# Four engines of a fused attention and MLP kernel kept in source order through seven batches, and a store moved by one slot

## The chip, the cores and the metric

The kernel runs on one core of a Trainium2 chip. The metric is the device time of one execution in microseconds (us). TensorE is called PE here, VectorE DVE, ScalarE ACT and SyncE SP, as the profile calls them; PEld is PE's loading of weights, which overlaps its matmuls.

## The reference

For 8 batches of 8 heads, 576 tokens and 64 dimensions, 32 packed queries `p` attend to the keys and values, and then every token attends to the 32 packed results. The heads are put side by side (4608 tokens of 512 values) and go through two MLPs, the first with a maximum of three projections, the second with a softplus.

```python
def sm_attn(qq, kk, vv):
    s = scale * np.matmul(qq, kk.transpose(0, 1, 3, 2))
    a = np.exp(s - np.max(s, axis=-1, keepdims=True))
    return np.matmul(a / (np.sum(a, axis=-1, keepdims=True) + 1e-09), vv)
packed = sm_attn(p, k, v)
x = heads_side_by_side(sm_attn(q, packed, packed))       # (4608, 512)
h = np.maximum(np.maximum(x @ w1, x @ w2), x @ w3)       # (4608, 768)
x = h @ w_out                                            # (4608, 512)
h = x @ w_in                                             # (4608, 2048)
g = np.maximum(h, 0.0) + np.log1p(np.exp(-np.abs(h)))
out = g @ w_out2                                         # (4608, 512)
```

The weights arrive as 64-bit floats and are narrowed to 32 bits on the chip.

## The kernel before

**Products.** A 32-bit operand is split into a high part (ACT, L106) and a low part (DVE, L107), and each product is three matmuls (`three`, L395: high by high, high by low, low by high). `split` is the helper that makes the two parts; its rows carry the names of what is split: `pwhi`/`pwlo` the packed weights, `hhi`/`hlo` the output of layer 1, `wc` the weights of the tail.

**A batch.** The second attention and layer 1 are one product: `packed_weights` (L374, tile `ps_w`, called PW below) multiplies the packed result of a batch by the weights of layer 1, 4 column blocks of 128 at a time (PW 0 to PW 4), and DVE and ACT split them. Then `layer1_unit` multiplies them by the attention weights `a2hi`/`a2lo`. A unit (f, w) is 12 matmuls; w is one of the three projections. ACT copies unit w = 0 out of PSUM (`m`, L418), and DVE takes the maximum with units 1 and 2 (L420). Layer 2 has four parts e, each 36 matmuls over f = 0 to 5, an ACT copy (L452) and a store to `x2d`.

**The slots.** Batches 1 to 7 run in a loop, ten slots each. Slot f = 0 to 5 has the three units of f; slots 6 to 9 have layer 2. Between the units of batch n lies the small work of batch n+1 (`small_work`): the first attention's scores (tiles `ps_s`; DVE takes the row maximum `mx`, L261, and scales it to `ms`, L265; ACT takes the exponential `e`, L270, with its sum, of which DVE makes `sg` and `rc`, L314 and L318), PE's transposes of `e` (tile `ps_e`, L285, copied by ACT to `e1T`, L291), the values (L305), the second attention's scores, and DVE's 32x32 transposes of the keys and queries (L219, L222). All PSUM tiles of the loop come from one pool of four.

**Narrowing.** Batches 1 to 6 also narrow the second MLP's weights, one block of 128 x 512 in each of the slots 0 to 5 (`narrow_ahead`): a load of a 64-bit block (`raw`, L651, three blocks ahead), ACT's `rebase` (L82) and DVE's two steps of `narrow` (L93, L96) into a tile `x` of a pool of three, which `store_narrowed` sends to DRAM from SP (L637).

**Batch 7** has no next batch and no narrowing. Instead it begins the tail (`BATCH_END`): `make_pair` forms sums of a weight block (four DVE steps `wu`, L717), splits them into `wc` (one ACT and one DVE step over 128 x 1792) and stores them to `wic`; `load_x2` and `make_x2` do the like for the first tokens.

**The tail** computes layers 3 and 4 in 9 chunks by 8 pairs (L812, L858 to L860). From the second pair on it reads each pair's `wc` two ahead, from `wic` (`get_pair`, L883).

**Order.** The instructions pass through a scheduler, which chooses each engine's order. PE's is fixed by `pinned`, which makes each step issue after the step before it; SP's transfers are likewise fixed by `in_turn` in the loop. DVE and ACT are free: the scheduler sets their instructions by its own estimates. A slot is written in this order:

```python
if 1 <= slot <= F1:
    layer1_split(n, slot - 1)
...
    for w in range(3):
        small_work(n, 3 * slot + w)
        pinned(layer1_unit, n, slot, w)
...
        transpose_kq(n + ahead, g, which)
...
        in_turn(load_raw, n + ahead, g, which)
store_narrowed()
if 0 < n < B - 1 and slot < F1:
    narrow_ahead()
```

The functions that the diff touches:

Of the kernel before, what the change touches and what calls it, by code (L numbers as in the profile page):

```python
# [19 lines left out]
def packed_attention_maxout_softplus(  # L20
# [35 lines left out]
    F1 = DF1 // P  # L56
# [563 lines left out]
    in_flight, to_store = [], []  # L620
# [4 lines left out]
    def in_turn(fn, *args):  # L625

        if queued:
            with tc.issue_after(queued[-1]):
                fn(*args)
        else:  # L630
            fn(*args)
        queued.append(last_of(mybir.EngineType.SP))

    def store_narrowed():
        while to_store:
            dst, x = to_store.pop(0)
            in_turn(lambda: nc.sync.dma_start(out=dst, in_=x))  # L637

# [24 lines left out]
        9: [("make", 1), ("load", 4), ("load", 5)],  # L663
    }

    for n in range(1, B):
        for slot in range(F1 + KC):

# [15 lines left out]
            for at, ahead, g, which in loads:  # L684
                if at == slot and n + ahead < B:
                    in_turn(load_raw, n + ahead, g, which)
            store_narrowed()
            if 0 < n < B - 1 and slot < F1:
                narrow_ahead()
            if n + 1 == B:  # L690
# [87 lines left out]
                        )(*args)  # L778
                if slot == F1 - 1:
                    wsb_ctx.close()  # L780
    aps_ctx.close()
    a_ctx.close()

# [163 lines left out]
```

## Time and profile before

| | us |
|---|---|
| median of 3 runs (1291.14 to 5892.78) | 1291.52 |
| the profiled execution | 1288.91 |
| its span, from the first to the last instruction | 1287.1 |
| PE busy | 1250.0 (97%) |
| PEld busy | 1127.7 (88%) |
| DVE busy | 719.4 (56%) |
| ACT busy | 458.2 (36%) |

The span's first 121 us hold the loads of the first batches and the whole of batch 0; batches 1 to 7 lie between 121.0 and 528.9, the tail behind that. Batches 1 to 6 repeat with a period of 59.20 us, so one of them is read for all; batch 4, from 298.6 to 357.8, is taken. Times of rows are those of the profiled execution. Spans of instructions that follow each other closely overlap by some hundredths of a microsecond, so that the distance of two starts is a little less than the span.

### The profile page before, as it was taken

To read this page: it belongs to the slowest core of one execution; us is meant where nothing else is said; L and a number is where in the kernel's file an instruction comes from. 1 tells how busy PE (TensorE), PEld (TensorE's weight loads), DVE (VectorE), ACT (ScalarE), POOL (GpSimd) and SP (SyncE) were. 2 spreads that over 40 slices of the span, in tenths; PEclk is the share of its full clock that TensorE was granted. 3 is DMA by queue.
4 is the path that set the end of the run, shared out by engine and by line. 5 is a ranking of instruction groups with operands and counts; after the bars stand their busy time and mean duration, and the time that the engine had idled before them with its cause. 6 is when DMAs were issued, how large, how long until landed. Compare 5 with 4: busy or idle time off the path is not lost.

```text
span 1287.1 us, 23495 instructions
## 1 busy us (share of the span) xinstructions
PE 1250.0 (97%) x9952; PEld 1127.7 (88%) x9952; DVE 719.4 (56%) x1115; ACT 458.2 (36%) x669; POOL 0.7 (0%) x6
## 2 busy tenths in 40 slices
PE   3889999999999999999999999999999999999998
PEld 2679898998989899999999999999999999999997
DVE  3777777786857657686354443544434445444332
ACT  3553434444343434553323323232232222332221
POOL 0000000000000000000000000000000000000000
PEclk7899999999999999999999999999999999999999
DMA  9972848677685724977646556565465554654651
GB/s 263 240 212 91 204 136 231 174 212 193 185 231 171 201 87 166 343 257 266 225 172 225 187 208 214 187 215 212 180 208 203 205 205 172 228 188 180 213 182 58
DMA packets 82121, 255.10 MB, mean 198 GB/s; under 512 B 12128, under 2 KB 47200, under 8 KB 72544
## 3 DMA queue, kind: packets, MB, share of 16 engines
q1 hardware_dynamic: 76240, 242.46, 59.1%
q10 hardware_dynamic: 5776, 11.14, 2.5%
q8 instruction: 78, 1.28, 0.4%
q14 instruction: 27, 0.22, 0.1%
HBM read 211.62 MB, written 41.94 MB: 197 GB/s over the span
## 4 chain that ended last, share of the span: by engine, by line
PE 81%; DVE 2%; DMA 1%; issue 0%; ACT 0%; SPq 0%; DVEq 0%
PE ps L812 28%; PE ps L395 21%; PE acc L860 10%; PE acc L859 10%; PE acc L858 10%; PE ps_w L374 2%; DMA wc<-wic 1%; PE ps_v L305 1%; PE ps_e L285 1%; DVE pwlo L107 1%; DVE mx L261 0%; PE ps_s L246 0%; DVE m L420 0%; DVE x L96 0%; DMA qraw<-in_q_dram 0%
## 5 line engine op out<-in xcount | busy, mean ns | idle before, releaser
L812 PE MATMUL ps<-x2hi,wc 128*128 128x256 f32 x2016 | 370.6, 282 | 0.8 <-DMA wc<-wic 0.8
L812 PEld LDWEIGHTS ps<-x2hi,wc 128*128 128x128 f32 x2016 | 316.1, 190 | 3.9 <-DMA wc<-wic 1.3
L812 PE MATMUL ps<-x2lo,wc 128*128 128x256 f32 x1008 | 283.7, 281 | 0.0
L860 PE MATMUL acc<-w2hi,glo 128*128 128x512 f32 x576 | 224.9, 391 | 0.0
L859 PE MATMUL acc<-w2lo,ghi 128*128 128x512 f32 x576 | 224.8, 390 | 0.0
L858 PE MATMUL acc<-w2hi,ghi 128*128 128x512 f32 x576 | 224.3, 389 | 0.0
L812 PEld LDWEIGHTS ps<-x2lo,wc 128*128 128x128 f32 x1008 | 191.4, 190 | 2.8
L841 ACT ACTIVATE h<-h 128x1024 f32<-128x1024 f32 x72 | 76.3, 1059 | 286.3 <-DVE h L838 286.3
L835 DVE TENSOR_TENSOR h<-h,ps 128x512 f32<-128x512 f32 x72 | 49.5, 687 | 227.8 <-PE ps L812 227.8
L107 DVE TENSOR_TENSOR glo<-h,ghi 128x1024 fp32r<-128x1024 f32 x72 | 88.1, 1223 | 85.1 <-ACT ghi L106 85.0
L395 PE MATMUL ps<-a2hi,pwhi 128*128 128x288 f32 x576 | 129.2, 306 | 2.9 <-DVE pwlo L107 0.9
L860 PEld LDWEIGHTS acc<-w2hi,glo 128*128 128x128 f32 x576 | 108.1, 188 | 23.0 <-DVE glo L107 0.2
L858 PEld LDWEIGHTS acc<-w2hi,ghi 128*128 128x128 f32 x576 | 108.3, 188 | 20.3
L859 PEld LDWEIGHTS acc<-w2lo,ghi 128*128 128x128 f32 x576 | 108.1, 188 | 20.5
L395 PE MATMUL ps<-a2lo,pwhi 128*128 128x288 f32 x576 | 123.8, 297 | 0.3 <-DVE a2lo L107 0.3
L395 PE MATMUL ps<-a2hi,pwlo 128*128 128x288 f32 x576 | 123.6, 296 | 0.0
L395 PEld LDWEIGHTS ps<-a2hi,pwhi 128*128 128x128 f32 x576 | 91.8, 189 | 17.9 <-ACT m L418 5.9
L834 ACT ACTIVATE h<-ps 128x256 f32<-128x256 f32 x72 | 27.5, 382 | 188.0 <-PE ps L812 188.0
L420 DVE TENSOR_TENSOR m<-ps,m 128x576 f32<-128x576 f32 x96 | 72.4, 755 | 38.8 <-PE ps L395 31.4
L395 PEld LDWEIGHTS ps<-a2lo,pwhi 128*128 128x128 f32 x576 | 93.1, 190 | 0.6 <-DVE a2lo L107 0.5
L395 PEld LDWEIGHTS ps<-a2hi,pwlo 128*128 128x128 f32 x576 | 93.0, 190 | 0.2 <-DVE pwlo L107 0.2
L107 DVE TENSOR_TENSOR pwlo<-ps_w,pwhi 128x512 fp32r<-128x512 f32 (+1 forms) x80 | 50.5, 631 | 67.1 <-ACT pwhi L106 66.6
(87 smaller groups left out, 1473.8 us busy)
## 6 DMA issues: line engine op xcount, KB each, us to landing
wc<-wic SPq DMA_DIRECT2D x66, 1792.0 KB
qraw<-in_q_dram SPq DMA_DIRECT2D x112, 140.0 KB
wic<-wc SPq DMA_DIRECT2D x8, 1792.0 KB
kraw<-in_k_dram SPq DMA_DIRECT2D x96, 140.0 KB
wraw<-in_moe_w_dram SPq DMA_DIRECT2D x18, 512.0 KB
x2d<-xs ACTq DMA_DIRECT2D x32, 288.0 KB
xu<-x2d SPq DMA_DIRECT2D x36, 256.0 KB
out_dram<-o SPq DMA_DIRECT2D x136, 64.0 KB
```

The source lines that it names most:

```text
L107: nc.vector.tensor_tensor(out=lo, in0=src, in1=hi.bitcast(F32), op=ALU.subtract)
L285: nc.tensor.transpose(ps[: 32 * TI, i // hi, (i % hi) * P : (i % hi) * P + P], e[:, i], ident,)
L374: nc.tensor.matmul(ps[cols, G, : units * P].rearrange("p (w x) -> p w x", w=units), ppT[n][rows, cols], wsb[rows, 4 * c : 4 * c + units, g ...
L395: nc.tensor.matmul(o, w, xx, start=first, stop=last)
L420: nc.vector.tensor_tensor(out=m, in0=ps[:, :, :HS], in1=ms[n, f], op=ALU.max)
L812: nc.tensor.matmul(out, l, r, start=(i == 0), stop=(i == len(terms) - 1))
L834: nc.scalar.activation(out=h[:, 3], in_=pa[:, 0], func=AF.Copy)
L835: add(out=h[:, 0:5:4], in0=h[:, 3:4].to_broadcast([P, 2, HC]), in1=pb, op=ALU.add)
L841: nc.scalar.activation(out=g, in_=g, func=AF.Softplus)
L858: nc.tensor.matmul(ps, ghi[:, i, cols], whi, start=first, stop=False)
L859: nc.tensor.matmul(ps, ghi[:, i, cols], wlo, start=False, stop=False)
L860: nc.tensor.matmul(ps, glo[:, i, cols], whi, start=False, stop=last)
```

## The change

The loop over batches 1 to 7 is put into a stretch in which the scheduler keeps PE, DVE, ACT and SP in the order in which the program is written. In `store_narrowed`, a block is stored while more than `left` blocks wait: in slots 0 to 5 one stays behind, so that a block narrowed in slot s is stored in slot s+2 rather than s+1, and slot 6 stores what is left.

```diff
-    def store_narrowed():
-        while to_store:
+    def store_narrowed(left):
+        while len(to_store) > left:
             dst, x = to_store.pop(0)
             in_turn(lambda: nc.sync.dma_start(out=dst, in_=x))
...
+    E = mybir.EngineType
+    order_ctx = tc.manual_schedule(engines={E.PE, E.DVE, E.Activation, E.SP})
+    order_ctx.__enter__()
     for n in range(1, B):
         for slot in range(F1 + KC):
...
-            store_narrowed()
+            store_narrowed(1 if slot < F1 else 0)
...
+    order_ctx.__exit__(None, None, None)
```

No instruction is added or removed on any engine. PE's order in the loop stays; 36 of its rows move where the tail begins.

DVE in batch 4, from unit (1,2)'s maximum to the split of PW 3, before:

```order
L420 TENSOR_TENSOR m_3972<-ps_1_3959,m_3910 128x576
L265 TENSOR_SCALAR ms_3954<-mx_3952 128x1
L314 TENSOR_SCALAR sg_4219<-es_3950 128x1
L318 RECIPROCAL rc_4221<-sg_4219 128x1
L107 TENSOR_TENSOR hlo_3989<-m_3972,hhi_3988 128x576
L314 TENSOR_SCALAR sg_4224<-es_3957 128x1
L318 RECIPROCAL rc_4226<-sg_4224 128x1
L420 TENSOR_TENSOR m_4020<-ps_1_4007,m_4005 128x576
L420 TENSOR_TENSOR m_4035<-ps_1_4022,m_4020 128x576
L219 STREAM_TRANSPOSE vT_3974<-qraw_3855 128x576
L107 TENSOR_TENSOR hlo_4046<-m_4035,hhi_4045 128x576
L107 TENSOR_TENSOR pwlo_4050<-ps_w_4051,pwhi_4049 128x512 x2
```

And after:

```order
L420 TENSOR_TENSOR m_3974<-ps_1_3961,m_3912 128x576
L219 STREAM_TRANSPOSE vT_3976<-qraw_3857 128x576
L93 TENSOR_SCALAR raw64_3473<-raw64_3473 128x512
L96 SCALAR_TENSOR_TENSOR x32_3983<-x32_3983,raw64_3473 128x512
L107 TENSOR_TENSOR hlo_3990<-m_3974,hhi_3989 128x576
L420 TENSOR_TENSOR m_4021<-ps_1_4008,m_4006 128x576
L420 TENSOR_TENSOR m_4036<-ps_1_4023,m_4021 128x576
L219 STREAM_TRANSPOSE vT_3976<-qraw_3862 128x576
L93 TENSOR_SCALAR raw64_3548<-raw64_3548 128x512
L96 SCALAR_TENSOR_TENSOR x32_4040<-x32_4040,raw64_3548 128x512
L107 TENSOR_TENSOR hlo_4047<-m_4036,hhi_4046 128x576
L107 TENSOR_TENSOR pwlo_4051<-ps_w_4052,pwhi_4050 128x512 x2
```

Two narrowings (L93, L96) and one more transpose of queries (L219) now stand between that maximum and the split of PW 3, and both row maxima and both `ms` ahead of it; before, these narrowings stood elsewhere in the batch, and `sg` and `rc` here.

ACT at the same place, from the copy of unit (2,0) to that of unit (3,0), before:

```order
L418 ACTIVATE m_4005<-ps_1_3992 128x576
L106 ACTIVATE hhi_4045<-m_4035 128x576
L106 ACTIVATE pwhi_4049<-ps_w_4051 128x512
L291 ACTIVATE e1T_4071<-ps_e_4064 96x768
L106 ACTIVATE pwhi_4049<-ps_w_4051 128x512
L291 ACTIVATE e1T_4080<-ps_e_4073 96x768
L418 ACTIVATE m_4095<-ps_1_4082 128x576
```

And after:

```order
L418 ACTIVATE m_4006<-ps_1_3993 128x576
L82 ACTIVATE x32_4040<-raw64_3548 128x512
L106 ACTIVATE hhi_4046<-m_4036 128x576
L106 ACTIVATE pwhi_4050<-ps_w_4052 128x512 x2
L291 ACTIVATE e1T_4072<-ps_e_4065 96x768
L291 ACTIVATE e1T_4081<-ps_e_4074 96x768
L418 ACTIVATE m_4096<-ps_1_4083 128x576
```

The copy of the first tile of transposes, `e1T`, moved behind the second `pwhi`.

DVE in batch 7, slots 2 and 3, from the last two maxima of slot 2 to the first of slot 3, before:

```order
L420 TENSOR_TENSOR m_6335<-ps_1_6322,m_6320 128x576
L717 TENSOR_TENSOR wu_6220<-wu_6220 128x256 x3
L107 TENSOR_TENSOR hlo_6351<-m_6335,hhi_6350 128x576
L717 TENSOR_TENSOR wu_6220<-wu_6220 128x256
L107 TENSOR_TENSOR pwlo_6355<-ps_w_6356,pwhi_6354 128x512
L107 TENSOR_TENSOR wc_6341<-wu_6220,wc_6341 128x1792
L107 TENSOR_TENSOR pwlo_6355<-ps_w_6356,pwhi_6354 128x512
L420 TENSOR_TENSOR m_6397<-ps_1_6384,m_6382 128x576
```

And after:

```order
L420 TENSOR_TENSOR m_6337<-ps_1_6324,m_6322 128x576
L720 TENSOR_TENSOR wu_6222<-wu_6222 128x256 x4
L107 TENSOR_TENSOR wc_6343<-wu_6222,wc_6343 128x1792
L107 TENSOR_TENSOR hlo_6353<-m_6337,hhi_6352 128x576
L107 TENSOR_TENSOR pwlo_6357<-ps_w_6358,pwhi_6356 128x512 x2
L420 TENSOR_TENSOR m_6399<-ps_1_6386,m_6384 128x576
```

The whole of `make_pair` (L720 is L717 before) now stands ahead of slot 3's splits.

SP's transfers in batch 4, slots 1 to 3 (`wi32` and `wo32` are the stores of narrowed blocks), before:

```order
L157 DMA qraw_3976<-in_q_dram 32x1120 x4
L637 DMA wi32_62<-x32_3870 128x4x128
L651 DMA raw64_3986<-in_moe2_w_out_dram 128x1024
L637 DMA wo32_64<-x32_3982 128x512
L651 DMA raw64_4043<-in_moe2_w_out_dram 128x1024
```

And after:

```order
L157 DMA qraw_3978<-in_q_dram 32x1120 x4
L651 DMA raw64_3987<-in_moe2_w_out_dram 128x1024
L637 DMA wi32_62<-x32_3872 128x4x128
L651 DMA raw64_4044<-in_moe2_w_out_dram 128x1024
L637 DMA wo32_64<-x32_3983 128x512
```

Each store moved behind one more load. Where the tail begins, SP's order changes too: the load of `wc` for pair 2 stands ahead of the loads of layer 4's weights, behind which it stood before, and the DVE part of `make_pair(1)`, which stood at the end of batch 7, stands behind the first drain of layer 3.

## Rows read from the trace of the kernel before

**Rows 1.** The page, busy time, share of the span and instructions of each engine.

```profile
PE 1250.0 (97%) x9952; PEld 1127.7 (88%) x9952; DVE 719.4 (56%) x1115; ACT 458.2 (36%) x669; POOL 0.7 (0%) x6
```

**Rows 2.** Window of batch 4: us, PE, PEld, DVE, ACT, POOL, PEclk, DMA share, GB/s.

```profile
298.60:357.80 59.20, 58.88 (x616) 53.04 (x615) 43.40 (x76) 24.79 (x44) 0.00 (x0) 1.00 0.73 200
```

**Rows 3.** The chain of waits in batch 4: start, us, what.

```profile
317.43 1.02 PE ps_w L374 x16
318.45 1.45 PE ps_e L285 x12
319.89 6.38 PE ps L395 x48
326.28 0.59 PE ps_w L374 x16
326.87 1.48 PE ps_v L305 x96
...
336.62 1.13 PE ps_s L246 x32
```

**Rows 4.** The timeline, batch 4, slots 1 and 2: start, us, engine, [idle before <-releaser].

```profile
309.45 0.42 DVE L93 TENSOR_SCALAR raw<-raw 128x512 int32<-128x512 int32 x1
...
310.43 0.68 DVE L96 SCALAR_TENSOR_TENSOR x<-x,raw 128x512 int32<-128x512 int32 x1
...
311.18 0.69 DVE L107 TENSOR_TENSOR pwlo<-ps_w,pwhi 128x512 fp32r<-128x512 f32 x1
...
311.79 1.41 DVE L261 TENSOR_REDUCE mx<-ps_s 128x1 f32<-128x576 f32 x2
...
312.02 0.51 PE L395 MATMUL ps<-a2hi,pwhi 128*128 128x288 f32 x2 [0.18 <-DVE pwlo L107]
...
313.12 0.14 DVE L265 TENSOR_SCALAR ms<-mx 128x1 f32<-128x1 f32 x1
...
313.18 0.74 DVE L420 TENSOR_TENSOR m<-ps,m 128x576 f32<-128x576 f32 x1
...
313.98 0.54 PE L395 MATMUL ps<-a2hi,pwhi 128*128 128x288 f32 x2
```

**Rows 5.** The timeline, batch 4, slots 2 and 3.

```profile
318.97 0.76 DVE L107 TENSOR_TENSOR hlo<-m,hhi 128x576 fp32r<-128x576 f32 x1
319.32 0.80 ACT L291 ACTIVATE e1T<-ps_e 96x768 f32<-96x768 f32 x1
...
319.65 0.68 DVE L107 TENSOR_TENSOR pwlo<-ps_w,pwhi 128x512 fp32r<-128x512 f32 x1
...
320.36 0.60 ACT L106 ACTIVATE pwhi<-ps_w 128x512 fp32r<-128x512 f32 x1 [0.24 <-DVE pwlo L107]
```

**Rows 6.** The timeline, batch 7, slots 2 and 3, DVE and ACT.

```profile
493.94 1.08 DVE L717 TENSOR_TENSOR wu<-wu 128x256 f32<-128x256 f32 x3
...
496.06 1.70 ACT L106 ACTIVATE wc<-wu 128x1792 fp32r<-128x1792 f32 x1 [0.84 <-DVE wu L717]
...
497.79 2.03 DVE L107 TENSOR_TENSOR wc<-wu,wc 128x1792 fp32r<-128x1792 f32 x1 [1.17 <-ACT wc L106]
...
498.14 0.65 ACT L418 ACTIVATE m<-ps 128x576 f32<-128x576 f32 x1
```

**Rows 7.** The timeline where layer 3 begins.

```profile
526.62 2.03 DVE L107 TENSOR_TENSOR wc<-wu,wc 128x1792 fp32r<-128x1792 f32 x1 [1.77 <-ACT wc L106]
...
536.41 0.38 SPq L883 DMA_DIRECT2D wc<-wic  x1
...
545.44 0.39 PE L812 MATMUL ps<-x2hi,wc 128*128 128x256 f32 x1 [0.83 <-DMA wc<-wic]
```

**Rows 8.** Windows where PE stands still in batch 0, columns as in Rows 2.

```profile
80.00:82.00 2.00, 0.00 (x0) 0.00 (x0) 1.95 (x5) 0.71 (x2) 0.00 (x0) 1.00 1.01 160
...
84.00:86.00 2.00, 2.00 (x10) 2.00 (x10) 0.00 (x0) 0.39 (x1) 0.00 (x0) 0.50 0.83 233
```

**Rows 9.** Window of 20 us from slot 2 of batch 4, columns as in Rows 2.

```profile
312.00:332.00 20.00, 19.85 (x252) 17.95 (x253) 13.76 (x28) 8.45 (x16) 0.00 (x0) 1.00 1.05 282
```

## The prediction

> **What bounds the kernel now.** Read the page's busy times first: PE is busy for 1250.0 of 1287.1 us, DVE for 56%, ACT for 36% [rows 1]. One batch is then read as a stretch of its own. Batch 4 takes 59.20 us, and PE's records cover 58.88 of it [rows 2]. That reads as if 0.32 us could be won, but a matmul that waits between two others is drawn longer, so PE's work is better counted. The chain of waits gives unstalled prices: 48 layer matmuls in 6.38 us, 0.133 each; a PW of 16 matmuls 0.59 to 1.02; transposes 1.45; values 1.48; scores 1.13 [rows 3]. A batch has 18 units of 12 matmuls and 4 parts of layer 2 of 36, so 360 x 0.133 = 47.9. With five PW (about 4.5), two scores (2.3), transposes, values and two small transposes (0.2) the sum is 57.8 us. **PE waits for at most some 1.4 us in each batch** (0.8 to 1.9 by the ends of a PW's price). That is the most which a better order could give back: 1.4 x 7 = 9.8 us, 0.8% of the run.
>
> The Trainium skill says the same of busy time: in Perfetto Trace Analysis, Identifying the Most-Contended Engine, the share of matmul busy time is called a poor measure of how near TensorE is to its limit, since pipelined instructions look smaller. The trace agrees in that a small gap hides some more waiting (0.32 against 1.4 us); by the busy time alone the gain would end at 2 us in all.
>
> Of the waits two can be placed. Unit (2,0) starts 0.18 us after PE had stopped, behind DVE's `pwlo`, and unit (2,1) at 313.98, when unit (1,2)'s maximum, 313.18 to 313.92, had freed its PSUM tile [rows 4]. The time between neighbours shows about 0.3 us lost at each. DVE is late there because it runs both row maxima (1.41 us) first, and because narrowing steps of 0.42 and 0.68 stand between the two `pwlo` [rows 4].
>
> **The change, part by part.** No work is added, so each term is a wait.
>
> *Slots 1 and 2, unit (2,1).* From the end of `pwlo` at 311.87 DVE now does maximum, `ms`, maximum, `ms` and then unit (1,2)'s maximum. The pieces are 0.70, 0.14, 0.70, 0.14 [rows 4] and some hundredths of handover, so that it starts near 313.6 rather than 313.18. The narrowing ahead is gone from here, which lets `pwlo` and with it unit (2,0) come no later. I take 0.25 us gained to 0.3 lost at this pair of waits, and choose a gain of 0.3, by the narrowing that left the chain.
>
> *Slots 2 and 3, unit (3,1), the term that decides.* Follow DVE through the after order from 313.6, with distances of starts, which for a pass over 128 x 576 is 0.68 (`hlo` at 318.97, the next at 319.65) [rows 5] and for L93 and L96 a few hundredths under the spans [rows 4]: unit (1,2)'s maximum 0.68, query transpose 0.69, L93 0.37, L96 0.65, `hlo` 0.68, and it is 316.7. Then two maxima (1.36), another query transpose (0.69), L93 and L96 (1.02) and `hlo` (0.68) end at 320.4, where the first `pwlo` of PW 3 starts; in the trace it starts at 319.65 [rows 5]. ACT's second `pwhi` waits for that first `pwlo` (start 320.36, released by `pwlo`) and takes 0.60 [rows 5], so now it ends near 321.7. Behind it in ACT's queue, no longer ahead of it, stands the copy `e1T` of the first transposes, 0.80 us, which ended at 320.12 [rows 5] and would now end near 322.45. Unit (3,1) takes the PSUM tile which that copy frees: its first matmul waits for ACT in both orders. Unstalled it would start 12 x 0.133 = 1.6 us behind unit (3,0), which starts at 319.89 less the 0.3 of above [rows 3], at about 321.2 at the latest and 321.0 by my replay. So PE stops for about 1.65 us. Less the 0.3 gained, a batch costs **+1.3 us**. Bounds: 0 if DVE catches up in the gaps that it has while PE does unit (2,1), up to 2.3 if the second `pwlo` (0.69 more) also holds unit (3,2). Five batches, 2 to 6, have narrowing in these slots ahead of them; batch 1 has none in flight yet and gains its 0.2. The sum is **5 x 1.3 = +6.5**, from -1.5 to +11.
>
> The Trainium skill states in PSUM — Partial Sum Buffer, Engine vs sequencer instructions, that the queues of ScalarE and VectorE are strictly first in, first out. By it the copy can't pass the waiting `pwhi`, and the 1.65 us stand; could it pass, this term would be -0.3 x 5. No row of before has a ready copy behind a waiting `pwhi`.
>
> *Batch 7.* The whole of `make_pair` for pair 2 now precedes slot 3's splits. Three of the four sums take 1.08 us, the ACT part 1.70 and the DVE part 2.03 [rows 6]. From the last maximum's end at 493.94: four sums to 495.4, ACT to 497.1, DVE to 499.1, `hlo` 499.8, the first `pwlo` 500.45, the second `pwhi` 501.1. The copy of unit (3,0), which ran at 498.14 [rows 6], is behind that on ACT and ends at 501.75 rather than 498.8; unit (4,0), due at about 499.15, waits for its tile. That is +2.6 us. In slot 4 pair 3 does the same in a smaller way (layer 2's first part waits for the last `hlo`): +0.5. Together **+3.1**, from 0 to 5.
>
> *Stores.* They issue one load later. That costs nothing while the store lands before ACT needs the tile back (a rival below).
>
> *The tail.* `make_pair(1)`'s DVE part, 526.62 to 528.6 before [rows 7], now follows the first drain of layer 3: ready about 6.5 us into layer 3, wanted at 5.0, so +1.1. Against it the load of `wc` for pair 2, issued at 536.41 behind other loads, held PE for about 1.0 us at 545.44 [rows 7]; it is now ahead of them: -1.0. Sum 0, within 2.
>
> *Clock.* In batch 0 PE stood still through 80 to 82, and the granted clock was 0.50 (1.2 of 2.4 GHz) at 84 to 86, with PE busy throughout [rows 8]. The stop in batch 7 is of that order (2.6 us). A fall like that one, some 1.7 us at half and partial speed, is possible: 0 to 1.7, I take +0.8. Stops of 1.65 us I price without it.
>
> **Sum:** 6.5 + 3.1 - 0.2 + 0 + 0.8 = +10. The profiled execution, 1288.91 us (1.8 over its span), becomes 1299; on the median of 1291.52 about **1301 us**, 0.8% slower. A measurement here tells about 2% from no change, so this counts as the same.
>
> **Rivals.**
> *The order gives back waits and the new ones don't come.* DVE is busy for 43.40 of 59.20 us [rows 2], so there is slack into which my chain of eleven steps may fit, above all if the steps are closer than their starts suggest. Then about 0.6 a batch and the 1.0 of the tail are won: 1291.5 - 4.2 - 1.0 = 1286; the limit is 9.8, 1282. Against it: ACT's copy stands behind a split which needs DVE's last step. Chance 0.13.
> *Nothing much moves*: unit (3,1) waits only 0.3 to 0.5 us, which the gain at (2,1) pays, and batch 7 costs 1 to 3: 1288 to 1295, mid 1292. Chance 0.19.
> *The stores become the bound, slower by over 2%.* Pool `x` has three tiles, so ACT's rebase of slot 3 needs the store of slot 0, now issued in slot 2, about 317.5. The DMA share is 1.05 from 312 to 332 [rows 9]. ACT can wait until about 4 us after its turn near 323.7 before PE feels it. A store that lands at 328 decides nothing; one that waits until the stretch ends at 332 costs 4.1 x 5 = 20.5 on top of the forecast's 10: 1321, +2.3%. Against it: the store has 11 us for a quarter of a megabyte while the core moves 282 GB/s [rows 9], and no L82 of batch 4 waits for a store. Chance 0.07.
>
> **How the numbers follow.** The forecast (+4 to +16) has 0.61, the rivals 0.13, 0.19 and 0.07. The range leaves out half of the gain's case and all of the stores': 1285 to 1313. Over 2% faster (1266) is beyond the limit of 9.8 us, 0.01; over 2% slower needs the stores or a fall of the clock in every batch, 0.08; the rest, 0.91, is within 2%.
>
> **What would show it.** In the profile of the changed kernel: batch 4 near 60.5 us rather than 59.20; unit (3,1) released by ACT's `e1T`, with PE idle before it; `e1T` behind two `pwhi`; no row L96 on the chain between the two `pwlo`; in batch 7 a stop of 2 to 3 us before unit (4,0), perhaps a clock below 1.00 behind it; the batch 7 stretch 55 to 57 us rather than 52.6; pair 2's `wc` no longer releasing PE in the tail. I am wrong if batches are under 59.2, if unit (3,1) starts without a wait, or if ACT's L82 waits for a DMA store.

## The result, and the profile after

The changed kernel takes **1304.33 us** (median of 6 runs, 1302.39 to 1306.58). The kernel before takes 1290.34 us beside it, the median of five runs, since a sixth, of 5892.78 us, is left out here and in the ratio. The ratio is 1.0109 with a 95% interval of 1.0095 to 1.0123: 14.0 us slower. The forecast was 1301, in a range of 1285 to 1313. The profiled execution has a span of 1301.7 us, 14.6 more than before.

The page's busy times, in the columns of [rows 1]:

```profile
PE 1255.7 (96%) x9952; PEld 1130.8 (87%) x9952; DVE 729.4 (56%) x1115; ACT 459.4 (35%) x669; POOL 0.7 (0%) x6
```

No engine got other work, as the counts show. So the loss must be waiting, or PE at a lower clock. The table of what PE waited for, over batches 1 to 7 and the tail's start (line waited for: us in total, times, longest us), says for whom. Before:

```profile
PE ps L395 <- DVE pwlo L107: 0.9, 5, 0.2
PE ps L812 <- DMA wc<-wic: 0.8, 1, 0.8
PE ps L395 <- DVE ms L265: 0.6, 1, 0.6
```

And after:

```profile
PE ps L395 <- ACT e1T L291: 7.9, 6, 1.8
PE ps L395 <- ACT m L418: 2.5, 1, 2.5
PE ps L816 <- DVE wc L107: 1.2, 1, 1.2
PE ps L395 <- DVE pwlo L107: 1.1, 6, 0.2
PE acc L862 <- ACT ghi L106: 0.8, 1, 0.8
PE ps L395 <- DVE hlo L107: 0.3, 1, 0.3
```

The first two rows of after are waits for ScalarE, the least busy of the three computing engines. Read from the starts of layer 2's last ACT copy in each batch, the batches compare so:

| us | batch 1 | 2 | 3 | 4 | 5 | 6 | 7 | tail |
|---|---|---|---|---|---|---|---|---|
| before | 59.19 | 59.25 | 59.19 | 59.20 | 59.26 | 59.20 | 52.57 | 758.1 |
| after | 59.41 | 62.50 | 60.63 | 60.62 | 60.82 | 60.62 | 57.63 | 759.9 |

Batches 3 to 6 give up 5.8 us together, batch 2 3.3, batch 7 5.1, the tail 1.8; batch 0 was 1.6 shorter in this execution. Sum: +14.6. Batch 0 lies ahead of the changed loop, and it took between 118.1 and 124.4 us in the executions profiled for this document; so profiles are compared below batch by batch, and not by their spans.

**The stop before unit (3,1).** Timeline of the changed kernel in batch 4, slots 2 and 3 (lines in between left out):

```profile
319.92 1.61 DVE L420 TENSOR_TENSOR m<-ps,m 128x576 f32<-128x576 f32 x2
...
321.41 1.52 PE L285 MATMUL ps_e<-ident,e 128*96 128x128 f32 x12
321.45 0.77 DVE L219 STREAM_TRANSPOSE vT<-qraw 128x576 f32<-128x576 f32 x1
...
322.14 0.39 DVE L93 TENSOR_SCALAR raw<-raw 128x512 int32<-128x512 int32 x1
322.16 0.58 ACT L106 ACTIVATE pwhi<-ps_w 128x512 fp32r<-128x512 f32 x1
...
322.64 0.69 DVE L96 SCALAR_TENSOR_TENSOR x<-x,raw 128x512 int32<-128x512 int32 x1
...
323.25 0.75 DVE L107 TENSOR_TENSOR hlo<-m,hhi 128x576 fp32r<-128x576 f32 x1
...
323.92 0.68 DVE L107 TENSOR_TENSOR pwlo<-ps_w,pwhi 128x512 fp32r<-128x512 f32 x1
...
324.63 0.60 ACT L106 ACTIVATE pwhi<-ps_w 128x512 fp32r<-128x512 f32 x1 [1.90 <-DVE pwlo L107]
325.13 1.50 ACT L291 ACTIVATE e1T<-ps_e 96x768 f32<-96x768 f32 x2
...
325.98 0.53 PE L395 MATMUL ps<-a2hi,pwhi 128*128 128x288 f32 x2 [1.46 <-ACT e1T L291]
```

The reader is to see ACT's empty time: it is done with the first `pwhi` at 322.74, and the transposes `ps_e` are there at 322.93, so the copies `e1T` could have run then, as they did before [rows 5]. They stand in the queue behind the second `pwhi`, which waits 1.90 us for DVE's `pwlo`. DVE reaches it only at 323.92, after two maxima, a transpose, L93, L96 and `hlo`. PE waits for `e1T` from 324.5 on.

By the source the second `pwhi` uses nothing of the first `pwlo`: the two calls of `split` read and write different halves of the same tiles. It waits all the same, before [rows 5] as after. No run here shows why, and none gave each half a tile of its own.

The length of the stop is told better by the starts of units (3,0) and (3,1) than by PE's idle time. Before, and after:

```profile
319.65 0.52 PE L395 MATMUL ps<-a2hi,pwhi 128*128 128x288 f32 x2
...
321.32 0.42 PE L395 MATMUL ps<-a2hi,pwhi 128*128 128x288 f32 x2
```

```profile
322.68 0.52 PE L395 MATMUL ps<-a2hi,pwhi 128*128 128x288 f32 x2
...
325.98 0.53 PE L395 MATMUL ps<-a2hi,pwhi 128*128 128x288 f32 x2 [1.46 <-ACT e1T L291]
```

The distance grew from 1.67 to 3.30, by 1.63 us, of which the profile draws 1.46 as idle.

**The stop in batch 7.** ACT and DVE there, two answers of the timeline:

```profile
503.24 1.70 ACT L106 ACTIVATE wc<-wu 128x1792 fp32r<-128x1792 f32 x1 [4.16 <-DVE wu L720]
504.85 0.67 ACT L106 ACTIVATE hhi<-m 128x576 fp32r<-128x576 f32 x1
505.42 0.58 ACT L106 ACTIVATE pwhi<-ps_w 128x512 fp32r<-128x512 f32 x1
508.30 0.60 ACT L106 ACTIVATE pwhi<-ps_w 128x512 fp32r<-128x512 f32 x1 [2.30 <-DVE pwlo L107]
508.80 0.65 ACT L418 ACTIVATE m<-ps 128x576 f32<-128x576 f32 x1
```

```profile
504.98 2.02 DVE L107 TENSOR_TENSOR wc<-wu,wc 128x1792 fp32r<-128x1792 f32 x1 [1.77 <-ACT wc L106]
506.92 0.75 DVE L107 TENSOR_TENSOR hlo<-m,hhi 128x576 fp32r<-128x576 f32 x1
507.59 0.68 DVE L107 TENSOR_TENSOR pwlo<-ps_w,pwhi 128x512 fp32r<-128x512 f32 x1
```

It is the same pattern with a longer delay: `wc`, which stood between the two `pwlo` before, now holds DVE ahead of both up to 507.0, the second `pwhi` waits 2.30 us for `pwlo`, and the copy of unit (3,0) behind it keeps a PSUM tile that unit (4,0) needs.

**The clock.** Windows of 2 us behind the stop of batch 2, then behind that of batch 7, in the columns of [rows 2]:

```profile
202.00:204.00 2.00, 0.80 (x5) 0.81 (x6) 0.69 (x1) 2.00 (x4) 0.00 (x0) 0.91 1.04 218
204.00:206.00 2.00, 2.00 (x10) 2.00 (x10) 0.00 (x0) 0.39 (x1) 0.00 (x0) 0.50 0.99 290
...
512.00:514.00 2.00, 2.00 (x22) 1.38 (x7) 1.08 (x2) 1.12 (x3) 0.00 (x0) 0.50 0.12 11
```

After each, the granted clock was 0.50 (1.2 of 2.4 GHz) for some microseconds with PE busy throughout, as in [rows 8].

**The stores.** ACT's wait for the tile of a narrowed block, over the same stretch:

```profile
ACT x L82 <- DMA wi<-x: 4.7, 2, 3.5
```

The rebase waited for a store in batch 2 (3.5 us) and in batch 3 (1.2 us); before, no rebase of these blocks waited for one. PE has no wait in the rows behind either.

### The profile page after: what moved, and what is told of

It reads as the page before. It is cut to its first block, busy times and chain, and to the rows that moved or that the text cites. A ratio compares the mean times of both kernels' runs of the same rounds, so it can differ in the third digit from the quotient of the medians.

```text
span 1301.7 us, 23509 instructions
## 1 busy us (share of the span) xinstructions
PE 1255.7 (96%) x9952; PEld 1130.8 (87%) x9952; DVE 729.4 (56%) x1115; ACT 459.4 (35%) x669; POOL 0.7 (0%) x6
## 4 chain that ended last, share of the span: by engine, by line
PE 63%; DMA 2%; DVE 1%; ACT 0%; issue 0%; SPq 0%; DVEq 0%; ACTq 0%
PE ps L816 27%; PE acc L864 10%; PE acc L863 10%; PE acc L862 10%; PE ps L395 5%; DMA qraw<-in_q_dram 1%; DMA wc<-wic 1%; PE ps_w L374 0%; ACT wc L106 0%; DVE m L420 0%; DVE wu L720 0%; DVE hlo L107 0%; DVE wc L107 0%; DMA out_dram<-o 0%; PE ps_v L305 0%
## 5 line engine op out<-in xcount | busy, mean ns | idle before, releaser
L395 PE MATMUL ps<-a2hi,pwhi 128*128 128x288 f32 x576 | 130.7, 309 | 12.3 <-ACT e1T L291 7.9
L395 PE MATMUL ps<-a2lo,pwhi 128*128 128x288 f32 x576 | 124.5, 298 | 0.3 <-DVE a2lo L107 0.3
L395 PE MATMUL ps<-a2hi,pwlo 128*128 128x288 f32 x576 | 124.6, 298 | 0.0
L395 PEld LDWEIGHTS ps<-a2hi,pwhi 128*128 128x128 f32 x576 | 92.6, 191 | 28.8 <-issue 9.9
L395 PEld LDWEIGHTS ps<-a2lo,pwhi 128*128 128x128 f32 x576 | 93.7, 191 | 0.6 <-DVE a2lo L107 0.5
L395 PEld LDWEIGHTS ps<-a2hi,pwlo 128*128 128x128 f32 x576 | 94.0, 192 | 0.0
L395 PE MATMUL ps<-hhi,wo_hi 128*128 128x288 f32 x384 | 83.0, 298 | 0.2 <-ACT hhi L106 0.2
```

Of the source, the lines that this page charges most:

```text
L395: nc.tensor.matmul(o, w, xx, start=first, stop=last)
```

## The experiments

Each ratio is to the kernel before on the same chip, where that took 1288.97 to 1289.64 us; so losses are compared by the ratios and not by the times. The changed kernel's is 1.0109. Theory A is the prediction's: a copy that is ready stands on ACT behind a split that waits for a late DVE. Rivals: DVE's lateness alone (B); the stores and SP (C).

**The two copies `e1T` ahead of the second `pwhi`.** DVE's order is that of the changed kernel, ACT's differs by this exchange.

```diff
...
-        for G in range(NG):
-            split(ps[:, G, : units * P], hi[:, G, : units * P], lo[:, G, : units * P])
+        part(0)                       # part(G) is the split of half G
+        if later: pending.append(part)
+        else: part(1)
...
             for G in range(NG):
                 pinned(attn1_transpose, m, G)
+            pending.pop()(1)
...
```

> The changed kernel with one exchange on ScalarE: the two copies e1T go ahead of the second pwhi of PW 3, behind the first. Theory A (the stop before unit (3,1) needs both: DVE late and e1T queued behind the pwhi that waits for DVE): the 1.58 us wait for e1T in batches 2 to 6 goes, batches 3 to 6 take about 59.05 rather than 60.62 us, batch 2 also gets back the clock's fall, in sum -8 to -10: 1294 to 1296 us. Rival B (DVE's lateness alone stops PE, whatever ACT's order): the wait stays, now on pwlo's tile at unit (3,2), and the time stays within 2 us of 1304. Rival C (the store's place or SP's order): no change.

1295.58 us, ratio 1.0039 (1.0025 to 1.0053). The wait for `e1T` is gone, and nothing took its place at unit (3,2). Batch 4 in the window's columns, and the waits of the same stretch as above (the edit moves the lines, so that L395 and L418 are L404 and L427 here):

```profile
301.71:360.56 58.85, 58.67 (x616) 52.97 (x615) 44.81 (x78) 24.95 (x44) 0.00 (x0) 1.00 0.75 201
```

```profile
PE ps L404 <- ACT m L427: 2.9, 2, 2.6
PE ps L826 <- DVE wc L107: 1.3, 1, 1.3
PE acc L872 <- ACT ghi L106: 1.3, 1, 1.3
PE ps L404 <- DVE pwlo L107: 1.1, 6, 0.2
```

A batch now takes 58.85 to 58.94 us (batch 2: 59.78), 0.3 *less* than before. So the kept order does win 0.3 us, and the stop overrides it. The gain lies at unit (2,1), which in the changed kernel's batch 4 follows unit (2,0) by 1.68 us rather than 1.96; the wait of 0.18 before unit (2,0) stays. Rival B falls.

In batch 2 of this kernel a rebase waited 5.5 us for a store, and PE then 0.33 us for a copy that stands behind it on ACT. So the wait for a store can reach PE, as it did in this one batch.

```profile
ACT x L82 <- DMA wi<-x: 7.7, 3, 5.5
```

**Source order in batches 1 to 6 alone.**

```diff
     for n in range(1, B):
+        if n == B - 1:
+            order_ctx.__exit__(None, None, None)
...
```

> Source order kept in batches 1 to 6 alone; batch 7 and the start of the tail are left to the scheduler. Theory A: batch 7 back to about 52.6 from 57.63 us, the tail about 1.8 us shorter, batches 2 to 6 as in the changed kernel: 1304.3 - 6.9 = 1297.5 (1296 to 1299). If the cost were spread over all batches alike (a dearer form of every wait), only a seventh, about 2 us, would go: 1302.

1299.2 us, ratio 1.0059 (1.0040 to 1.0079), at the upper end of what was expected. Batch 7 is back at 52.57 and the tail at 758.4 us, batch 2 keeps 62.50 and batches 3 to 6 keep 60.63 to 60.93. The loss sits at the two places and isn't spread.

**Source order with the stores as before, and the later stores without it.**

```diff
-            store_narrowed(1 if slot < F1 else 0)     # changed kernel
+            store_narrowed(0)
```

> Source order of the four engines kept, but the stores one slot after the narrowing, as before. Theory A: the stores cost nothing here, 1304 within 1.5 us, the same wait for e1T. Rival C (the later store or its landing holds ACT's rebase): 3 us or more under the changed kernel. If the later store is what keeps SP from standing still: above 1306, with loads late.

> The kernel before with the stores two slots after the narrowing, and no kept order. Theory A: 1291 within 1.5 us, batches at 59.2. Rival C: 3 us or more above, with L82 or a load waiting for a DMA.

1304.69 us (1.0109, 1.0087 to 1.0132) and 1291.83 us (1.0014, 0.9999 to 1.0029). The loss comes with the kept order; the stores' place doesn't matter to it. By itself the later store costs 0.14%, some 2 us, with an interval that reaches nothing. In the profile batches 3, 4 and 6 of that kernel take 59.64 us, and PE waits for `pwlo` 2.7 us in 5 times, where the waits for `pwlo` came to 0.9 before. Batch 5 takes 60.94, with a wait of 1.05 us before the values (L305) that the profile puts down to no other engine. No wait of PE in those batches is put down to a transfer; the scheduler, given the stores elsewhere, chose a slightly different order on DVE and ACT.

**ACT left to the scheduler, DVE left to the scheduler, both left.**

```diff
-    order_ctx = tc.manual_schedule(engines={E.PE, E.DVE, E.Activation, E.SP})
+    order_ctx = tc.manual_schedule(engines={E.PE, E.DVE, E.SP})           # ACT free
+    order_ctx = tc.manual_schedule(engines={E.PE, E.Activation, E.SP})    # DVE free
+    order_ctx = tc.manual_schedule(engines={E.PE, E.SP})                  # both free
```

> The changed kernel with ScalarE left to the scheduler: PE, DVE and SP in source order, so DVE is as late as in the changed kernel, and ACT's order has e1T ahead of the second pwhi. Theory A: no wait for e1T, batches 3 to 6 about 59, the stop of batch 7 on DVE's make_pair staying: 1294 to 1297. Rival B (DVE's order alone): the wait stays and the time is within 2 us of 1304.

> The changed kernel with VectorE left to the scheduler: PE, ACT and SP in source order, so e1T stays behind the second pwhi. DVE's order then has no L93 between unit (1,2)'s maximum and the split of PW 3, but sg and rc and the two L96 are still there, and make_pair stays whole in batch 7. Theory A in the form that ACT's order is what turns DVE's lateness into a stop: the wait for e1T stays, 1.0 to 1.6 us in each of batches 2 to 6, the stop of batch 7 too: 1299 to 1304. If DVE's kept order is the cause: about 1291.

> The changed kernel with only PE and SP kept in source order, VectorE and ScalarE left to the scheduler; the later stores stay. Theory A: neither stop, batches at 59.2 and batch 7 at 52.6: 1289 to 1292. If SP's kept order costs something by itself: 1294 or more.

| kept | us | ratio (interval) | batch 4 | batch 7 | PE's wait for `e1T` |
|---|---|---|---|---|---|
| PE, DVE, ACT, SP | 1304.33 | 1.0109 (1.0095 to 1.0123) | 60.62 | 57.63 | 7.9 |
| PE, ACT, SP | 1302.11 | 1.0089 (1.0074 to 1.0104) | 60.26 | 57.63 | 5.3 |
| PE, DVE, SP | 1291.36 | 1.0019 (1.0007 to 1.0031) | 58.90 | 55.45 | none |
| PE, SP | 1291.53 | 1.0014 (1.0001 to 1.0028) | 59.57 | 52.57 | none |

The last row has the later stores in a free order, as above; its batches 3, 4 and 6 take 59.6 us, and batch 5 60.36 with the wait before the values again. Most of the loss hangs on **ACT's** order: with ACT free 0.19% is left of 1.09%. DVE is then as late as in the changed kernel (the first `pwlo` starts 21.65 us into batch 4, rather than 21.78), and batches 1 to 6 are the short ones of 58.9 us. With DVE free that `pwlo` still starts at 21.40, where it was 20.82 before, so that row doesn't show what a DVE in time would do; the next experiment does. With ACT free the time is under the expected 1294 to 1297, since even the stop of batch 7 shrinks: the scheduler put the copy of unit (3,0) ahead of the second `pwhi`. ACT and PE there:

```profile
493.34 1.70 ACT L106 ACTIVATE wc<-wu 128x1792 fp32r<-128x1792 f32 x1 [0.29 <-DVE wu L720]
494.95 0.63 ACT L418 ACTIVATE m<-ps 128x576 f32<-128x576 f32 x1
498.40 0.60 ACT L106 ACTIVATE pwhi<-ps_w 128x512 fp32r<-128x512 f32 x1 [2.83 <-DVE pwlo L107]
```

```profile
498.42 0.53 PE L395 MATMUL ps<-a2hi,pwlo 128*128 128x288 f32 x2 [0.85 <-DVE pwlo L107]
```

`pwhi` waits even longer, 2.83 us, but nothing that PE needs soon is queued behind it; PE loses 0.85 us, to `pwlo` itself. Batch 7 is still 2.9 us longer than before, so there a part of the loss stays with the kept order of DVE.

**Two narrowings left out on DVE.** The steps L93 and L96 of slots 1 and 2 in batches 2 to 6 aren't done; ACT's order stays.

```diff
             rebase(raw64, x)
-            narrow(raw64, x)
+            if not skip:                      # skip: n > 1 and slot in (1, 2)
+                narrow(raw64, x)
```

> The changed kernel with VectorE's two narrowing steps (L93, L96) left out for the blocks of slots 1 and 2 in batches 2 to 6, so those weights are not narrowed; ScalarE's order is unchanged. By theory A the first pwlo of PW 3 comes some 1.2 us earlier (not 2.1, since it then waits for pwhi), the wait for e1T falls from 1.58 to about 0.4 us, batches 3 to 6 take 59.3 to 59.5, and the clock no longer falls in batch 2: 1295 to 1299 us. If ACT's order alone makes the stop: 1303 to 1305.

1297.84 us, ratio 1.0063 (1.0045 to 1.0081). Batch 4, and PE's wait:

```profile
299.62:359.04 59.42, 58.98 (x616) 53.04 (x615) 42.94 (x74) 24.99 (x44) 0.00 (x0) 1.00 0.74 199
```

```profile
PE ps L395 <- ACT e1T L291: 1.5, 6, 0.3
```

With ACT's order unchanged the wait falls from 1.46 to 0.25 us a batch. The first `pwlo` starts at 20.57 in this batch, earlier than the 20.82 of before, so the 0.25 is what ACT's order costs with a DVE in time, and 1.2 us come of DVE's lateness on top of it. The whole stop needs both: a late DVE and a copy queued behind the split that waits for it. The cure on ACT removes the stop, that on DVE four fifths of it, and only the first leaves no work out.

**`make_pair` behind the next slot's splits in batch 7.**

```diff
...
+                    if n + 1 == B and w == 0 and late:     # pairs 2 and 3
+                        make_pair(late.pop())
...
```

> The changed kernel with batch 7's make_pair for pairs 2 and 3 moved from the end of slots 2 and 4 behind the first unit of slots 3 and 5, so that those slots' splits go first. Theory A: the 2.5 us stop before unit (4,0) and the 0.5 at layer 2 go, with the clock's fall behind them: batch 7 53 to 54 rather than 57.63 us, 1304.3 - 4 = 1300 (1299 to 1301.5), the e1T waits staying. Rival: a make_pair costs the same wherever it stands in source order, the stop moves to unit (4,1) or the next packed weights: 1303 to 1305.

1300.72 us, ratio 1.0096 (1.0082 to 1.0110). The time lies in the expected range, but by the ratio only 1.7 us are won, which isn't clear of noise, and the expected reason fails. Batch 7 took 58.51 us, more than before the move, with a fall of the clock behind the second of the stops below. What the profiled execution gained on the changed kernel's lies in batch 2, where the clock stayed up (61.00 rather than 62.50), and in a tail of 757.9 rather than 759.9. The rival holds for batch 7: the stop moved.

```profile
PE ps L395 <- DVE m L420: 2.1, 1, 2.1
PE ps L395 <- ACT hhi L106: 2.0, 1, 2.0
```

A `make_pair` holds DVE for about 5 us in source order, from its first sum to the end of `wc`, with DVE idle while ACT does its half. The scheduler filled that with `hlo` and `pwlo`: before, both ran ahead of `wc`'s start at 497.79 [rows 6]. A fixed order of whole steps can't, at either of the two places tried.

**Stores one slot later still.**

```diff
-            store_narrowed(1 if slot < F1 else 0)
+            store_narrowed(2 if slot < F1 else 0)
```

> The changed kernel with the stores one slot later still: a block of slot s is stored in slot s+3, just ahead of the rebase that needs its tile of the pool of three. This finds the point of the rival of the stores. If a store lands within 2 to 3 us of its issue, ACT's L82 waits that long in slots 3 to 5, with hhi behind it, and PE loses 0 to 2 us a batch more: 1304 to 1316. If stores land only when the loads of slots 2 to 5 are through (6 us and more), ACT's queue stands for that: 1325 or more.

1304.69 us, ratio 1.0108 (1.0091 to 1.0124): no loss, the lower end of what was expected. ACT waited for a store, both times in batch 2:

```profile
ACT x L82 <- DMA wi<-x: 7.2, 2, 4.1
```

PE's waits are those of the changed kernel, but for 0.5 us more for `ghi` in the tail. Even a rebase that waited 4.1 us for its tile didn't stop PE there. So the rival of the stores was worth nothing here, though not by a wide margin: behind 5.5 us, in the kernel with the two `e1T` exchanged, PE stopped for 0.33.

**The cures together, and a version that beats both.** Source order in batches 1 to 6, with the two `e1T` ahead of the second `pwhi`; then also the load of pair 2's `wc` ahead of the loads of layer 4's weights.

```diff
...
+                if i < 2:
+                    get_pair(*seq[i + 2])
                 if c == 0:
...
-                if i + 2 < len(seq):
+                if 2 <= i and i + 2 < len(seq):
                     get_pair(*seq[i + 2])
```

> Both cures at once: source order in batches 1 to 6 alone, with the two e1T copies ahead of the second pwhi. If the two places of theory A hold all of the loss, batches 1 to 6 take 58.92 us as measured with that exchange, against 59.20 before, batch 7 52.6 and the tail as before: 1289.6 - 6 x 0.28 = about 1288, between 1286 and 1290. If a third loss is hidden in the kept order, 1293 or more.

> The kernel of six_e1t with the load of pair 2's wc issued ahead of the loads of layer 4's weights at the tail's start. In the kernels before PE waited there 0.8 to 1.8 us for that load. Gain of the load's place: 0.5 to 1.8 us under six_e1t, about 1287; none if the load waits for its buffer rather than for the queue.

1287.41 us (0.9990, 0.9979 to 1.0001) and 1285.47 us (**0.9972**, 0.9960 to 0.9984). Batches 2 to 6 are at 58.9, batch 7 at 52.6. Batch 1 is at 60.4 and 60.9, with a stop of 1.25 and 1.72 us before a unit of layer 1. The profile puts it down to DVE steps that run at the same place, with no stop behind them, in the kernel with the exchange alone; its cause isn't shown. PE's waits where the tail begins; for the first of these kernels

```profile
PE ps L827 <- DMA wc<-wic: 0.7, 1, 0.7
```

and for the second none. The second is faster than the kernel before by 3.5 us, its interval clear of 1. That the last step alone is worth 1.9 us isn't shown: the two intervals overlap.

## Why the prediction was right

**The forecast, step by step.** *Unit (2,1):* a gain of 0.3 was taken; the kernels without the stop show 58.9 against 59.2. Right. *Unit (3,1):* a stop of 1.65 us was forecast and 1.63 measured in batch 4 by the starts of the units, 1.46 by idle time (1.81 in batch 2). The replayed chain was met in its distances, shifted by the batch's start: from the end of the second maximum to `pwlo` 2.4 us in the trace, and 2.4 by the steps. The mechanism is right, and five such stops appeared, as forecast. The size is partly luck: the prediction's own times, 322.45 for the copy's end less 321.0 to 321.2 for the unstalled start, make 1.25 to 1.45, and no row that it names gives the 0.2 that it wrote on top. With the gain it made 1.3 a batch; batches 3 to 6 lost 1.42 to 1.56. That `e1T` can't pass the waiting `pwhi` is what the Trainium skill's PSUM — Partial Sum Buffer (Engine vs sequencer instructions) states of ScalarE's queue; the trace agrees, with 2.2 us between the end of the transposes and the copy. The prediction says that no row of before has a ready copy behind a waiting `pwhi`; the trace of before does have one, since the second `e1T` of batch 4 ran behind the `pwhi` that waited 0.24 us [rows 5].

*Batch 7:* 2.6 forecast for the stop before unit (4,0), 2.55 measured; 0.5 at layer 2, 0.49 measured. Of the batch's loss of 5.1 us these are 3.0, the clock (below) is 1.5, and half a microsecond isn't placed. *Batch 1:* -0.2 forecast, +0.22 measured, small and wrong in its sign: there too PE waited for `e1T`, 0.23 us.

**What was too small.** The forecast's +10 became +14.0, and +14.6 in the two profiled executions. By the batches of these two, the stops at unit (3,1) cost 7.7 us for 6.5, batch 7 without its clock 3.6 for 3.1, batch 1 0.4 more than forecast, and batch 0, which wasn't in the sum, gave 1.6 back. Two terms were far off. *The clock:* 0.8 us was put in for batch 7 and nothing for the five shorter stops. In the profiled execution it fell after the stops of both batches 2 and 7. Its price is read from pairs with nearly the same stop: batch 2 took 62.50 where the clock fell and 61.07 in the kernel with the stores as before, where it didn't; batch 7 took 57.63, and 56.15 with a like stop and the clock at 1.00. That is 1.4 and 1.5 us, 2.9 together, against 0.8. *The tail:* 0 was forecast with 2 either way, +1.8 measured. The first term of it, DVE's late `wc`, was written as 1.1 (6.5 less 5.0 would be 1.5) and measured as 1.2. The gain from the earlier load of pair 2 did come (0.2 of waiting instead of 0.8, where 1.0 was forecast), but a wait of 0.8 for ACT's `ghi`, which the sum didn't have, took it.

**The limit and the signs.** The prediction bounds PE's waiting in a batch by 0.8 to 1.9 us; with five PW at 0.59 its own sum ends at 2.9. No kernel here came near either end: the shortest full batch of any kernel here takes 58.85 us, 0.35 under the 59.20. The 1.4 us that it sets beside the gap of 0.32, as an agreement of the trace, was its own estimate. What the runs do show of idle time that leaves out some waiting is the stop of 1.63 us with 1.46 idle. Of the signs that were named, batch 4, the releaser of unit (3,1) and the stop in batch 7 came as written. Batch 7, at 57.6 us, is over the 55 to 57, and the load of pair 2 still held PE for 0.2. One sign of being wrong came too: ACT's L82 did wait for a store, without a stop of PE behind it.

**The rivals.** The rival of a gain counted 0.6 us a batch without the new stop; the cured kernels show half of that, 0.3. That the new waits would be absorbed is refuted by the rows. The stores decided nothing in time. They don't always land before their tile is needed, but PE felt it only behind waits of 5.5 us and more.

**One thing not settled:** why the clock fell behind batch 2's stop of 1.81 us in the changed kernel and stayed up behind one of 1.81 in the kernel with `make_pair` moved and one of 1.88 in the kernel with the stores as before, no run here tells.

## What to carry to other kernels

An engine with a third of its time in use can set the pace through its order: look, on every in-order queue, for a ready instruction behind one that waits for another engine, and follow who needs it. Keeping source order does well where the source says what is urgent, and badly where a helper issues a whole step, such as both halves of a split or a sum with its split, in one piece; break such a step where the other engine's wait lies. When a change has a good part and a bad one, find which engine's order the loss hangs on by freeing one engine at a time, and then by the one exchange that should cure it.

## What the runs showed of the hardware

Whether a stop of PE is followed by a fall of the granted clock differs between executions with nearly the same stop. Behind batch 2's stop it fell to 0.50 in the changed kernel, and in those with source order in batches 1 to 6 and with the stores one slot later still. It stayed at 1.00 with `make_pair` moved, and in the kernel with the stores as before, whose windows show PE as idle as in the changed kernel's:

```profile
204.00:206.00 2.00, 0.91 (x7) 0.91 (x8) 0.69 (x1) 2.00 (x4) 0.00 (x0) 1.00 1.08 314
206.00:208.00 2.00, 2.00 (x18) 2.00 (x17) 0.76 (x1) 0.96 (x2) 0.00 (x0) 1.00 1.08 374
```

Behind the stop of 2.5 to 2.6 us in batch 7 it fell in five of the six kernels that had it. It never fell behind the stops of 1.46 us in batches 3 to 6 of the changed kernel. Each fall in batches 2 and 7 cost 1.4 to 1.5 us, on top of stops of 1.8 and 2.5.
